# One step list per tile rewritten, one more filler product behind each early burst, one weight load issued elsewhere

## The chip, the cores and the metric

The kernel runs on one core of a Trainium2 chip. Its metric is the time of one execution on the device in microseconds (us), taken as the median of several runs. A separate profiled execution gives the trace that is quoted here; its times count from the first instruction of the program.

A core has five engines that run side by side, each through its own instructions in order: PE (TensorE, matrix products; its weight loads are shown as PEld), DVE (VectorE), ACT (ScalarE), POOL (GpSimd) and SP, which here only issues DMAs. They meet at semaphores. PE writes to PSUM, in banks; DVE and ACT read PSUM and write SBUF.

## The reference

The first half is a linear-attention recurrence with decay, for 4 batches, 8 heads, 768 steps and head size 48. Per batch and head, with a 48x48 state:

```
y[t]  = r[t] @ (state + (u * k[t]) outer v[t])
state = w[t][:, None] * state + k[t] outer v[t]
```

The second half takes the 3072 tokens by 384 features that come out of it through a two-layer network: `gelu(x @ w_in) @ w_out`, with 2048 hidden features and the exact gelu. The inputs r, k, v, w, u are float32; w_in and w_out are float64 and are reduced to float32 on the chip.

## The kernel before

**Tiles.** The 3072 tokens are cut into eight tiles of 384. For each tile `attention(x, unit)` does the recurrence in chunks of 64 steps, and `mlp(x)` does the network. Both are Python generators: each `yield` ends a piece, a handful of instructions. A loop over x runs the pieces of tile x's attention beside those of tile x-1's network; after the eighth tile the last network runs alone.

**The order of work is written by hand.** No scheduler moves anything: instructions stand on each engine in the order in which the Python code emits them. `PLAN[x]` is a string with one letter per piece. For x = 0: `.` and `s` step the two units of tile 0's attention (unit 0 and unit 1, half of the heads each), `f` begins tile 1's attention, `c` steps the conversion of the weights, `l` the loads, `w` loads v of tile 1. From x = 1 on: `.` steps `mlp(x-1)`, `s` the rest of `attention(x)`, `f` the beginning of `attention(x+1)`, `l` the loads of the next tile, `c` the conversion (tile 1 only), `x` sums of the inputs of `mlp(x)`, and `w` sums of weights, on DVE. What a string leaves over is run at its end; a letter whose generator is used up does nothing.

**Tile 0.** Here no network runs yet. Each unit goes through six levels (h = 1, 2, 4, 8, 16, 32). At each, `products` (L473) puts a burst of 24 small products on PE, DVE copies the wanted part of the result to `a_sb` (L569, masked) and scales r and k in place for the next level (L540, L551). Behind most bursts `keep_warm(1)` (L235) issues one product of zeros, 512 columns in bf16, whose result nobody reads. Then come the transposes of k (L742), which ACT copies out (L755), the products k v (L792, `kv_ps`), the chain of states on DVE (L824, L819), the products inside a chunk (L845) and those with the states (L888), both into `y_ps`, the fences on DVE (L855, L858), and the copies to `xT` (L895, L911, L914), the network's input. Tile 1's first burst is L489. The network of tile 0 then begins at L1278.

**Weights.** The weights come in 16 pieces of 768 KB, the first eight of w_in. `weight_in(i)` loads piece i into one of five `raw` buffers: with a gate in three DMAs, each ahead of it on DVE a memset of one element (L217) that makes SP wait for DVE, and without one in a single DMA (L213). `conversion()` turns piece i into float32: three ACT instructions a piece, made one piece ahead (L343, L344, L346), a shift on DVE (L355) and an addition on DVE (L359); behind the addition it calls `weight_in(i + 3)`, but not for piece 0. Piece 3 is therefore loaded by the `l` letters of tile 0, at the end of their chain:

```
"l": chain(weight_in(0, True), islice(second, 5), weight_in(1, True), weight_in(2, True), second, weight_in(3, True)),
```

`second` is `load_second`: eight loads of tile 1's r, k and w (L177), each behind a DVE memset (L176) as well.

**Tiles 1 to 7.** The network of tiles 0 and 1 uses L1278 for its first layer; from tile 2 on it is L1066, in fewer products (a two-level scheme with sums of weights and of inputs, L972 to L980 and L989). The second layer is L1372 in tile 0's network and L1292 otherwise. Its results leave by ACT and DVE (L1281, L1283 gelu in tile 0's network; L1411, L1415 for the output). PSUM for the network is two banks that change places, so a product waits for the reader of the one before the last. Attention's bursts from tile 2 on are L641 and L632.

Of the kernel before, what the change touches and what calls it, by code (L numbers as in the profile page):

```python
# [36 lines left out]
NC_SP = 8  # L37
HALFWAY = 2
PLAN = {
    0: ".lls.....sslsc.lsslll.sl.sls.f.sl.lfscsl..sfss.lscfs.lscs.s.sssscl..ls...ssslll.l.cs...sw.ccff",  # L40
    1: (
        ".cswc.ccc.cccss.lc.ccscs..cc.cs.cclwcsc.ccssc.c.cccsccc..ssccc.c.lcls.cc.ccsc.w.clwscclccc"
        ".c.swcw.ss.ccs.lcsc..cwcccslccslff..w..fw.wfs..f..flffffffww"
    ),
    2: "...l...s..ws.swssswssss.sslsw...ssss.sssws.ll..ws.w..lw.sw.wl.sls.sls..lf.s....sf..f.f.xx.fxl.x.x",
    3: "l..sss..s.s..s.s....s...s.ssllss.sss.s.s.ss.l..lsss..sssss.sls.s..s......s..ls.llssf.sf.sflf.f.x.x..xxfffxf",
    4: "...s...lsl......s.s....sss..ssss..s..ss..s..s...llssslss....s.slss...s...sll.sl.s.sfs..fsf.ff..xl.x.xfffxffx",
    5: ".l..........ls.ss...s.sslls.ssss..ss.sls...sss..sssssl.ss.s..s.......s.lssll.sfsf.f.s.ff.x..x.xxxl",
    6: "sss.sls.....s......ls.s....s.sssssss..s.....s.ss....s.s.ssss.s.l.ss.l.ls.l...s.l.lslssf..s.ffs..lff.xx..xffxffx",
    7: "......s.s....s.s...s.ssssss...sss.ss...sss..ssss.s...ss.ww.ww.wwsw.ww.ww.ws.s.ss.s.ww.swww.swwwwwwww.wwww.www.xxxx.xxxxxx",  # L50
}


# [11 lines left out]
def kernel(  # L65
# [47 lines left out]
    def pair(name):  # L113
        return pools["d"].tile([128, 2, BANK], F32, name=name, tag="d")
# [56 lines left out]
    def load_second(dma):  # L171

        loaded[1] = [None, None]
        for i in range(SHARES):
            s = slice(i * 3 * ALL // SHARES, (i + 1) * 3 * ALL // SHARES)
            nc.vector.memset(bufs[1][:, s.start:s.start + 1], 0.0)  # L176
            dma.dma_start(out=bufs[1][:, s], in_=rkw[1, :, s])  # L177
            yield

    def load(x, dma):  # L180

        if x >= NX:
            return
        loaded[x] = [None, None]
        for i in (0, 2, 1):
            t = bufs[x % 2 if i == 0 else 1]
            for j in range(3):
                a = i * ALL + j * ALL // 3
                dma.dma_start(out=t[:, a:a + ALL // 3], in_=rkw[x, :, a:a + ALL // 3])
                yield  # L190
        load_v(x, dma)
        yield
# [12 lines left out]
    def weight_in(i, gate=False):  # L205

        if i < len(pieces):
            dst, src = pieces[i]
            raws[i] = cv.tile([128, PIECE], I64, name="raw", bufs=AHEAD) if wide else None
            if wide:  # L210
                dst = raws[i].rearrange("p (a c) -> p a c", a=dst.shape[1])
            if not gate:
                nc.sync.dma_start(out=dst, in_=src)  # L213
                return
            for a in range(dst.shape[1]):
                if wide:
                    nc.vector.memset(dst[:, a].bitcast(U32)[:, 0:1], 0)  # L217
                nc.sync.dma_start(out=dst[:, a], in_=src[:, a])
                yield
# [12 lines left out]
    def keep_warm(n):  # L232
        t = ps.tile([128, BANK], F32, name="warm", tag="mm", bufs=2)
        for _ in range(n):
            nc.tensor.matmul(t, lhsT=zeros[:, 0:128], rhs=zeros, start=True, stop=True)  # L235
# [81 lines left out]
    def conversion():  # L317

        i = converted[0]
        if i >= len(pieces):  # L320
            return
        converted[0] += 1

        prepare(i + HALFWAY)
        yield
        if wide:
            yield from finish(pieces[i][0], raws[i], *halfway[i])
        for _ in weight_in(i + 3) if i else ():
            pass

    def convert():
# [3 lines left out]
    def prepare(upto):  # L335
        if not wide:
            return
        for i in range(len(halfway), min(upto, len(pieces))):
            words = raws[i].bitcast(U32).rearrange("p (a b) -> p a b", b=2)
            lo, hi = words[:, :, 0], words[:, :, 1]  # L340
            f = cv.tile([128, PIECE], U32, name="f")
            e = cv.tile([128, PIECE], U32, name="e")
            nc.scalar.activation(out=f.bitcast(F32), in_=hi.bitcast(F32), func=AF.Abs, scale=2.0 ** -112)  # L343
            nc.scalar.activation(out=e.bitcast(F32), in_=lo, func=AF.Identity, scale=2.0 ** -51, bias=two)  # L344
            sign = e.bitcast(F16).rearrange("p (a b) -> p a b", b=2)[:, :, 1]
            nc.scalar.activation(out=sign, in_=hi.bitcast(F32), func=AF.Copy, scale=2.0 ** -100)  # L346
            halfway.append((f, e))

    def finish(dst, raw, f, e):

        nc.vector.tensor_scalar(out=f, in0=f, scalar1=3, scalar2=None, op0=ALU.logical_shift_left)  # L355
        yield
        yield
        f, e = (z.rearrange("p (a c) -> p a c", a=dst.shape[1]) for z in (f, e))
        nc.vector.tensor_tensor(out=dst.bitcast(U32), in0=f, in1=e, op=ALU.add)  # L359
# [4 lines left out]
    def attention(x, unit):  # L364
# [101 lines left out]
        def products(bs, right, width, rest=False, last=False):  # L466
            d = pair("d")
            n = 0
            for b in bs:
                for i in range(NI):  # L470
                    for g in range(2):
                        for p in range(2):
                            nc.tensor.matmul(d[half[p], g, n * width:(n + 1) * width],  # L473
                                             lhsT=kc[half[g], b, i, p], rhs=right(half[g], b, i, p),
                                             start=True, stop=True)
                    n += 1
            if x == 0 and not rest and not last:
                keep_warm(1)
            return d[:, :, 0:n * width]

        def first_and_diagonal():
# [409 lines left out]
        if split:  # L891
            for c, copy in enumerate((nc.scalar.copy, nc.vector.tensor_copy)):
                for z in range(2):
                    s = slice(z * G, z * G + D)
# [5 lines left out]
        for b in reversed(range(np_)):  # L900
            for q in reversed(range(Q)):
# [5 lines left out]
                if which < NJ:  # L907
                    for z in range(2):
                        s = slice(z * G, z * G + D)
# [37 lines left out]
    def homes():  # L947

        more = [cv.tile([128, PIECE], I64, name="s", tag="raw", bufs=AHEAD).bitcast(F32) for _ in range(2)]
        s3_sb.append(more[0][:, 0:HF * 128].rearrange("p (f c) -> p f c", f=HF))  # L950
        x_sums.extend(z[:, i * HT:(i + 1) * HT] for z in (more[0][:, HF * 128:], more[1][:, HF * 128:]) for i in range(2))
        spare = [cv.tile([128, PIECE], F32, name=name) for name in ("f", "f", "e", "e")]
        for i, name in enumerate(("s1", "s2")):
            s12_of[name] = [z[:, 0:FG * 128].rearrange("p (f c) -> p f c", f=FG) for z in spare[2 * i:2 * i + 2]]
        s_both.extend((more[1], s_home))
        spare15.extend(z[:, FG * 128 + i * 128:FG * 128 + (i + 1) * 128] for z in spare[:1] for i in range(2))
        second = [more[1][:, i * WI:(i + 1) * WI] for i in range(HK)]
        third = [s_home[:, i * WI:(i + 1) * WI] for i in range(HK)]
        fourth = [z[:, FG * 128:] for z in spare]
        s_of.extend((second, third, fourth))  # L960
# [460 lines left out]
    second = load_second(nc.sync)  # L1421
# [8 lines left out]
    def next_v():  # L1430
        load_v(1, nc.sync)
        yield
# [7 lines left out]
    for x in range(NX):  # L1440
        if x == 2:
            homes()
        following = attention(x + 1, 0) if x + 1 < NX else iter(())
        if x == 0:
            streams = {
                ".": units[0], "s": units[1], "f": following, "c": pieces_of_w, "w": next_v(), "x": iter(()),
                "l": chain(weight_in(0, True), islice(second, 5), weight_in(1, True), weight_in(2, True), second, weight_in(3, True)),
            }
        else:
            streams = {  # L1450
                ".": mlp(x - 1), "s": slots, "f": following,
                "l": load(x + 1, nc.sync),
                "x": sums_of_x15(x) if x == NX - 1 else sums_of_x(x) if x > 1 else iter(()),
                "w": masks_and_sums() if x == 1 else chain(first_sum(), h_sums()) if x == 2 else sums_of_w15() if x == NX - 1 else iter(()),
                "c": pieces_of_w if x == 1 else iter(()),
            }
        for c in PLAN[x]:
            next(streams[c], None)
        for c in ".slxw" if x == 0 else ".slxwc":
            while next(streams[c], streams) is not streams:  # L1460
                pass
        slots = following
        if x == 1:
            fewer_pairs()
# [62 lines left out]
```

## Time and profile before

| What | us |
|---|---|
| Runs before | 586.98, 587.47, 590.91; median 587.47 |
| Profiled execution, its own time | 587.83 |
| Its span, first to last instruction | 585.9 |
| PE busy, of the span | 569.6 (97%) |
| DVE busy | 460.9 (79%) |
| ACT busy | 287.3 (49%) |
| PE busy in the first 30 us | 21.97 |
| PE busy from 30 to 60 us | 25.42 |
| First product of tile 0's network (L1278) | starts at 45.41 |

Some 1.9 us of the profiled execution's time lie outside its span. In a row of a timeline the columns are start, duration (both us), engine, line, operation, output<-input, shape and count; what stands in brackets is the idle time before the row and what ended it. "issue" there means that the engine waited for nothing that the profile shows. In a row of stretches the columns are the stretch, its length, the busy time of PE, PEld, DVE, ACT and POOL (instructions in brackets), the granted PE clock, the DMA engines' busy share, and GB/s. A float32 product is two rows of PE and two of PEld.

### The profile page before, as it was taken

To read this page: it belongs to the slowest core of one execution; us is meant where nothing else is said; L and a number is where in the kernel's file an instruction comes from. 1 tells how busy PE (TensorE), PEld (TensorE's weight loads), DVE (VectorE), ACT (ScalarE), POOL (GpSimd) and SP (SyncE) were. 2 spreads that over 40 slices of the span, in tenths; PEclk is the share of its full clock that TensorE was granted. 3 is DMA by queue.
4 is the path that set the end of the run, shared out by engine and by line. 5 is a ranking of instruction groups with operands and counts; after the bars stand their busy time and mean duration, and the time that the engine had idled before them with its cause. 6 is when DMAs were issued, how large, how long until landed. Compare 5 with 4: busy or idle time off the path is not lost. (4 is left out here: it accounts for less than half of the span.)

```text
span 585.9 us, 17174 instructions
## 1 busy us (share of the span) xinstructions
PE 569.6 (97%) x7405; PEld 507.1 (87%) x7408; DVE 460.9 (79%) x823; ACT 287.3 (49%) x672; POOL 8.0 (1%) x21
## 2 busy tenths in 40 slices
PE   7769999999999999999999999999999999999997
PEld 4556666766899999999999999999999999999997
DVE  7879766999969986787859987598768998975532
ACT  2566889322722558146463368245562465623400
POOL 4100000000000000000000000000000000000000
PEclk9899999999999999999999999999999999999999
DMA  7659661120142301341023311430015200210000
GB/s 248 207 146 349 239 207 56 37 86 2 32 138 79 111 2 32 97 126 39 1 42 104 122 39 19 96 118 5 3 30 166 73 3 2 43 39 7 1 15 34
DMA packets 51034, 46.78 MB, mean 80 GB/s; under 512 B 31760, under 2 KB 36112, under 8 KB 50960
## 3 DMA queue, kind: packets, MB, share of 16 engines
q1 hardware_dynamic: 50864, 45.62, 25.6%
q8 instruction: 58, 0.95, 0.7%
q14 instruction: 16, 0.13, 0.1%
q10 hardware_dynamic: 96, 0.07, 0.1%
HBM read 36.24 MB, written 4.72 MB: 70 GB/s over the span
## 5 line engine op out<-in xcount | busy, mean ns | idle before, releaser
L1066 PE MATMUL h_ps<-xT,w_in_sb 128*128 128x192 f32 x408 | 81.3, 330 | 0.7 <-DVE o_sb L1415 0.6
L1066 PEld LDWEIGHTS h_ps<-xT,w_in_sb 128*128 128x128 f32 x408 | 67.8, 190 | 3.7 <-ACT g L1098 1.2
L1278 PE MATMUL h_ps<-xT,w_in_sb 128*128 128x384 f32 x192 | 64.2, 490 | 0.1
L1278 PEld LDWEIGHTS h_ps<-xT,w_in_sb 128*128 128x128 f32 x192 | 35.8, 190 | 24.4 <-ACT rkw L1283 0.6
L1292 PE MATMUL o_ps<-w_out_sb,g 128*128 128x192 f32 x224 | 39.5, 326 | 0.0
L1292 PEld LDWEIGHTS o_ps<-w_out_sb,g 128*128 128x128 f32 x224 | 37.0, 190 | 0.3
L657 ACT COPY a_sb<-d 32x256 f32<-32x256 f32 (+8 forms) x90 | 32.6, 362 | 4.6 <-PE d L641 3.1
L1292 PE MATMUL o_ps<-w_out_sb,f 128*128 128x192 f32 x176 | 31.7, 330 | 0.0
L1292 PE MATMUL o_ps<-t,g 128*128 128x192 f32 x176 | 31.4, 329 | 0.0
L1292 PE MATMUL o_ps<-w_out_sb,e 128*128 128x192 f32 x176 | 31.3, 328 | 0.0
L1292 PE MATMUL o_ps<-t,e 128*128 128x192 f32 x176 | 30.9, 327 | 0.0
L1292 PE MATMUL o_ps<-t,s 128*128 128x192 f32 x176 | 30.9, 327 | 0.0
L1066 PE MATMUL u_ps<-s,w_in_sb 128*128 128x192 f32 x160 | 29.5, 327 | 0.0
L674 DVE COPY_PREDICATED a_sb<-quarter,d 128x480 f32<-128x480 uint8 (+5 forms) x54 | 23.2, 438 | 7.7 <-PE d L641 6.5
L1281 ACT ACTIVATE g<-h_ps 128x256 f32<-128x256 f32 (+1 forms) x32 | 13.8, 433 | 31.0 <-PE h_ps L1278 30.6
L1292 PEld LDWEIGHTS o_ps<-t,g 128*128 128x128 f32 x176 | 28.7, 190 | 0.4
L1292 PEld LDWEIGHTS o_ps<-w_out_sb,e 128*128 128x128 f32 x176 | 28.8, 190 | 0.3
L1292 PEld LDWEIGHTS o_ps<-w_out_sb,f 128*128 128x128 f32 x176 | 28.7, 190 | 0.4
L1292 PEld LDWEIGHTS o_ps<-t,s 128*128 128x128 f32 x176 | 28.8, 190 | 0.1
L1292 PEld LDWEIGHTS o_ps<-t,e 128*128 128x128 f32 x176 | 28.8, 190 | 0.1
L473 PEld LDWEIGHTS d<-rkw 64*64 64x64 f32 x1056 | 18.7, 142 | 11.2 <-issue 7.1
L641 PE MATMUL d<-kx,rkw 64*64 64x96 f32 x1056 | 28.2, 248 | 0.0
(247 smaller groups left out, 1185.6 us busy)
## 6 DMA issues: line engine op xcount, KB each, us to landing
rkw<-in_rkw_dram SPq DMA_DIRECT2D x54, 256.0 KB, 4.0
raw<-in_w_out_dram SPq DMA_DIRECT2D x8, 768.0 KB, 5.3
v_in<-in_v_dram SPq DMA_DIRECT2D x8, 584.0 KB, 4.0
out_dram<-o_sb SPq DMA_DIRECT2D x20, 192.0 KB, 1.9
rkw<-kx SPq DMA_DIRECT2D x72, 48.0 KB, 2.0
raw<-in_w_in_dram SPq DMA_DIRECT2D x12, 256.0 KB, 4.5
raw<-in_w_in_dram SPq DMA_DIRECT2D x4, 768.0 KB, 9.4
rkw<-in_rkw_dram SPq DMA_DIRECT2D x6, 384.0 KB, 5.5
```

Of the source, the lines that this page charges most:

```text
L473: nc.tensor.matmul(d[half[p], g, n * width:(n + 1) * width], lhsT=kc[half[g], b, i, p], rhs=right(half[g], b, i, p), start=True, stop=True)
L641: nc.tensor.matmul(o[half[p], i * 3 * C // 2:(i + 1) * 3 * C // 2], lhsT=kc[half[g], n // NI, n % NI, p], rhs=rx[half[g], 2 * n + p], star ...
L657: nc.scalar.copy(out=at[z, g, first:behind, (a + 1) * h:], in_=d[z, :, :, to] if g == slice(None) else d[z, :, to])
L674: nc.vector.copy_predicated(out=an[:, :, :, :, (a + 1) * h:], mask=mask.to_broadcast(data.shape), data=data)
L1066: nc.tensor.matmul(o, lhsT=lhsT, rhs=rhs, start=start, stop=True, skip_group_check=True)
L1278: nc.tensor.matmul(h_ps, lhsT=w_in_sb[:, f // FI, j, f % FI * 128:(f % FI + 1) * 128], rhs=xT[:, j, :], start=(j == 0), stop=(j == NJ - 1))
L1281: nc.scalar.activation(out=gs[group][:, f % FG, 0:t], in_=h_ps[:, 0:t], func=AF.Gelu)
L1292: nc.tensor.matmul(o, lhsT=lhs(j), rhs=rhs(j), start=start and j == 0, stop=(j == HF - 1), skip_group_check=True)
```

## The change

Three things change. `keep_warm(1)` in `products` becomes `keep_warm(2)`, for the ten bursts of tile 0 that had one. The load of weight piece 3 leaves the `l` chain and is issued, without a gate and in a single DMA, behind the addition of piece 0. All eight strings of `PLAN` are new: in tile 0 the letters but `l` stand as before and the last `l`s stand together and earlier; in tiles 1 to 7 the same pieces stand in another order, and the strings have a few letters more, which run what the end of the string ran before or do nothing.

```diff
 PLAN = {
-    0: ".lls.....sslsc.lsslll.sl.sls.f.sl.lfscsl..sfss.lscfs.lscs.s.sssscl..ls...ssslll.l.cs...sw.ccff",
+    0: ".lls.....sslsc.lsslll.sl.sls.f.sl.lfscsl..sfss.lscfs.lscs.s.ssssclll..s...sss..cs...sw.ccff",
     1: (
-        ".cswc.ccc.cccss.lc.ccscs..cc.cs.cclwcsc.ccssc.c.cccsccc..ssccc.c.lcls.cc.ccsc.w.clwscclccc"
-        ".c.swcw.ss.ccs.lcsc..cwcccslccslff..w..fw.wfs..f..flffffffww"
+        ".c.scccl..lscssc.cccscxcl..ccc.cscclcccc..ccscs.ccc.cc.ccss.cccccs.c.wcwccssss..c.ccss.ccl"
+        ".sswwww.cccccccslwcclllf....sslc...cc...sf.fs.ffff...fffwffwwwwwlc"
     ),
-    2: "...l...s..ws.swssswssss.sslsw...ssss.sssws.ll..ws.w..lw.sw.wl.sls.sls..lf.s....sf..f.f.xx.fxl.x.x",
+    2: "....s...slw.sswssl.sssss...ss.sss.swsllsslwsww...s...sl..www.wslss..lcs.s.lf.sl..fx.w.xxx....sxxfff.....l",
...
@@ conversion
-        for _ in weight_in(i + 3) if i else ():
+        for _ in weight_in(i + 3):
             pass
@@ products
             if x == 0 and not rest and not last:
-                keep_warm(1)
+                keep_warm(2)
@@ streams of x == 0
-                "l": chain(weight_in(0, True), islice(second, 5), weight_in(1, True), weight_in(2, True), second, weight_in(3, True)),
+                "l": chain(weight_in(0, True), islice(second, 5), weight_in(1, True), weight_in(2, True), second),
```

More of the change, by code (lines that the diff above doesn't have):

```diff
@@ L39 @@
 PLAN = {
-    0: ".lls.....sslsc.lsslll.sl.sls.f.sl.lfscsl..sfss.lscfs.lscs.s.sssscl..ls...ssslll.l.cs...sw.ccff",
+    0: ".lls.....sslsc.lsslll.sl.sls.f.sl.lfscsl..sfss.lscfs.lscs.s.ssssclll..s...sss..cs...sw.ccff",
     1: (
-        ".cswc.ccc.cccss.lc.ccscs..cc.cs.cclwcsc.ccssc.c.cccsccc..ssccc.c.lcls.cc.ccsc.w.clwscclccc"
-        ".c.swcw.ss.ccs.lcsc..cwcccslccslff..w..fw.wfs..f..flffffffww"
-    ),
-    2: "...l...s..ws.swssswssss.sslsw...ssss.sssws.ll..ws.w..lw.sw.wl.sls.sls..lf.s....sf..f.f.xx.fxl.x.x",
[L46 to L50, printed above, removed]
+        ".c.scccl..lscssc.cccscxcl..ccc.cscclcccc..ccscs.ccc.cc.ccss.cccccs.c.wcwccssss..c.ccss.ccl"
+        ".sswwww.cccccccslwcclllf....sslc...cc...sf.fs.ffff...fffwffwwwwwlc"
+    ),
+    2: "....s...slw.sswssl.sssss...ss.sss.swsllsslwsww...s...sl..www.wslss..lcs.s.lf.sl..fx.w.xxx....sxxfff.....l",
+    3: (
+        "wscl..ss..s..sss....s...l.s.ssssssss..s..l.ss...sss..sllssss.ss...s...s...s...sllsssllf.sl"
+        ".ff.fxxlx.xx....sffxfff"
+    ),
+    4: (
+        "......llls..ss.....s....sss..ssss.....llssss..s...ssss...s..lssc..ss.....ssllsss..lfs..lfs"
+        ".f..sffx..x.xffxxwfff.xl"
+    ),
+    5: ".......s...l.lls.s...s..ssssslssss...ss....sss.ssssss...s...ss...l.s..lslllfsss..c.sfffs..l..lwfxxx.xxx.",
+    6: (
+        "ss.ss....s...s....ss...s...sssls.slss....sss...s...ssss..lss...s..sscw....lll.ssll..sssslf"
+        "..sf.f.ffll.x..x.x.ffsffxxx"
+    ),
+    7: (
+        "......s..s...s.s...sss.ss.ss.sss..ss...wwwsss..swssswcs.ss.ww....l.s.wwwsww.wwww..ws.s.ss."
+        "s.wwwwwswwwwww.ww.xxxxxww..xxx.wwsxx.x"
+    ),
 }
```

## The prediction

> **What bounds the kernel.** I read the busy times first, then PE in thirty-microsecond stretches, since PE is busy for 97% of the span.
>
> ```profile
> PE 569.6 (97%) x7405; PEld 507.1 (87%) x7408; DVE 460.9 (79%) x823; ACT 287.3 (49%) x672; POOL 8.0 (1%) x21
> 0.00:30.00 30.00, 21.97 (x651) 15.09 (x654) 24.23 (x69) 12.42 (x20) 7.99 (x21) 0.94 0.69 227
> 30.00:60.00 30.00, 25.42 (x563) 18.37 (x562) 25.83 (x67) 20.60 (x42) 0.00 (x0) 1.00 0.74 253
> 60.00:90.00 30.00, 30.00 (x366) 18.85 (x365) 20.99 (x26) 26.14 (x45) 0.00 (x0) 1.00 0.59 202
> ```
>
> Of PE's 16.3 us without work, 12.6 lie before 60 us (8.03 + 4.58). From the start of tile 0's network (45.41) on, PE is full, and PE's list of waits from 60 us on has one line, 0.6 us behind the output's copies. So products can't be packed closer in tiles 1 to 7: their seven strings can lose time, and gain next to none. What can be gained lies before 45.41, and it moves the rest as a block. The second reading is therefore PE's timeline there.
>
> ```profile
> 36.47 0.39 PE L888 MATMUL y_ps<-rkw,st 64*64 64x64 f32 x5
> 38.19 1.09 PE L888 MATMUL y_ps<-rkw,st 64*64 64x64 f32 x30 [1.33 <-issue]
> ...
> 40.42 1.32 PE L888 MATMUL y_ps<-rkw,st 64*64 64x64 f32 x38 [0.27 <-DVE fence L855]
> ...
> 41.64 0.33 PE L489 MATMUL d<-kx,rkw 64*64 64x96 f32 x3
> 43.29 2.19 PE L489 MATMUL d<-kx,rkw 64*64 64x96 f32 x91 [1.32 <-issue]
> 45.41 0.91 PE L1278 MATMUL h_ps<-xT,w_in_sb 128*128 128x384 f32 x2
> ```
>
> Two stops with the word "issue" break rows that are otherwise back to back, in the middle of a group with its operands ready. A third stands in L473 (17.2 to 18.85, 1.42). Counted from the start of PE's rows, the three restarts are rows 703, 1727 and 1983: multiples of 256 apart. The queue that the page calls "instruction" moves records of 16 KB, and one ends 1.3 us before each restart (16.24 + 1.36, 35.92 + 0.96, 41.05 + 0.95). So I read them as PE out of instructions: a record follows PE's passing of a multiple of 256 and brings the next block but one. How long it takes hangs on the data. Block edges were passed at 28.06, 33.54 and 38.19; the records after the last two came 2.4 and 2.9 us later, and the DMA queues show why for the last:
>
> ```profile
> q1 hardware_dynamic: 529, 0.99, 92.2%
> q8 instruction: 1, 0.02, 5.9%
> ```
>
> The first line is 38.1 to 41 us, where the data queue alone appears; the second, from 41 to 42, is the record. Elsewhere, with quiet DMA engines, the record came 1.1 to 1.3 us behind the edge.
>
> **The load of piece 3.** It removes three DVE memsets (L217, 0.06 each) and two of three issues on SP, and takes 768 KB out of the time after 36.89, where SP issues them now:
>
> ```profile
> 36.89 1.33 SPq L218 DMA_DIRECT2D raw<-in_w_in_dram  x3
> 30.98 5.82 SPq L177 DMA_DIRECT2D rkw<-in_rkw_dram  x3
> ```
>
> It comes to stand on SP behind piece 2 and behind DVE's addition of piece 0 (29.98 to 30.93), with no wait for a buffer, five being there for the first five pieces. The `second` loads of the lower row now go at 30.98, 32.94 and 36.47; with the `l`s together they go at about 31. Piece 3 and the last of these, 0.77 + 0.29 MB at the 345 GB/s of 38.19 to 41, are 3.1 us of DMA. From 28.06 to 33.54 the engines are busy 48%, so 2.85 us are free, and 1.86 more up to 36.5. They fit, and 38.19 to 43.3 grows quiet.
>
> *Second stop* (41.64 to 43.29). The edge at 38.19 with a quiet record is 1.2 + 1.0 + 1.3 = 3.5 us, so 41.7, when PE is at that row: the stop goes. Without it L489's row follows 41.64 by some 0.09 instead of 1.65: −1.56. What is late next: the network waits for `xT` (L895 on ACT, ends at 43.43) and its DMAs, and L489's own rest (2.19) still covers that.
>
> *First stop* (36.86 to 38.19). The edge at 33.54 with a quiet record: 33.54 + 3.5 = 37.0, just in time; but that window now takes part of the moved bytes. And what follows is held by DVE: L888 of unit 0 needs the fences behind the state chain (L819, until 38.96), so it starts at 39.3 at best against 40.42, −1.1. Ends 0 and −1.1; I take the middle, −0.55, since the bytes end within a microsecond of that record.
>
> Sum of the load: **−2.1**. Ends 0 and −2.7, and a loss (the slower rival).
>
> **The second zero product.** Ten rows of 512 columns in bf16, 0.215 us each start to start at full clock, are 2.15 us of PE. They stand behind bursts after which PE waits for DVE or ACT (0.5 to 0.9 us: L551, L569, L566, L540 in PE's list of waits), so these waits hide them: 0. Uncovered it is +2.15. They could also earn: the clock was granted at half once, right behind a stretch of the same length in which PE worked 1.40 of 3.41 us.
>
> ```profile
> 15.97:19.38 3.41, 1.40 (x50) 1.01 (x49) 3.37 (x7) 3.26 (x5) 0.85 (x1) 1.00 0.52 130
> 19.39:22.80 3.41, 3.41 (x98) 2.80 (x97) 2.78 (x7) 1.10 (x4) 0.00 (x0) 0.50 1.02 342
> ```
>
> At half clock three bursts took 1.56, 1.51 and 1.39 instead of 0.93, 1.7 us in all, and DVE waited 0.36 + 0.54 + 0.64 for them. But two more zero rows there are 0.43 us, and the stop at 17.2, most of the idleness, has its record in flight already. And the gain wouldn't arrive: ACT stands until 25.64 for weight piece 1.
>
> ```profile
> 25.64 0.94 ACT L343 ACTIVATE f<-raw 128x768 f32<-128x768 f32 x1 [5.16 <-DMA raw<-in_w_in_dram]
> ```
>
> From there ACT goes nearly without pause (the conversion, L417/L419, eight L566 to 32.57, L755) to the products k v at 33.13. So I take 0; ends −1.5 and +2.15.
>
> [...] The ten products are also 20 more PE rows, so the edges fall up to 20 rows earlier in the work: about 0.3 us in a stop's favour, within the ends.
>
> **Plans 1 to 7.** Products and their number are the same; what changes is which piece stands ahead of which. *Tile 1:* ACT carries the conversion (three instructions, 2.8 to 3.0 us a piece, rows 35.34 to 38.25) besides gelu (L1281, 0.44), and PE takes six rows of L1278 per hidden block (64.2 us over 192 rows), 2.0 us. In the new order one more conversion stands ahead of a gelu whose bank PE wants two blocks later; 2.9 + 0.44 against the 4.0 of two blocks leaves cover, but where ACT is late already a little is lost: **+0.15**, ends 0 and +1.5 (half a conversion uncovered). *Tiles 2 to 7:* the distance on PE from a tile's products k v to the next tile's first burst, in products of 0.326 us, is 94, 114, 90, 86, 86, 86 before and 100, 110, 90, 86, 86, 86 now. Twice the change puts more products between the output's copies and the bank's next use, where the 0.6 us of waits are, so some 0.4 can go; DVE's spare time at the seam of tiles 2 and 3 falls from 1.2 us to about none. **−0.2**, ends −1.1 and +0.7.
>
> **Sum.** 587.83 − 2.1 + 0 + 0.15 − 0.2 = 585.7 against the profiled execution's own time (span 585.9 and 1.9 around it), which is 0.36 above the runs' median of 587.47. I state **585.6**.
>
> **Rivals.**
> 1. *The stops stay* as they are, since the data's bytes were not what delayed the records: only the strings' terms are left, 587 to 588.3. For it speaks that stops also occur at 17.2 with DMA engines busy but 52%. Against it the 92.2% and 1.1 to 1.3 us elsewhere. [...]
> 2. *The clock's gain arrives too*, or both stops go entirely: a further 1.1 to 2.1, 583.5 to 584.5.
> 3. *Slower: the moved bytes delay the earlier record.* With 3.1 us pushed into 28 to 36.5, the block after 33.54 comes later than 38.19. It decides once that record starts after 35.92. At the 2.9 us seen under 92% it starts at 36.45, +0.5, and with piece 3's tail still there up to 1.7 more at both stops: 588.3 to 589.5.
> 4. *Tile 1 starves:* gelus behind conversions uncovered by half a conversion or more at two or more blocks, +1.5 to +4: 589.5 to 592.
>
> **Chances.** Forecast (584.5 to 586.9) 50%, no gain 20%, clock 10%, late record 12%, tile 1 8%. The range takes the first four but for the tails: 583.6 to 589.0. A measurement of this kernel tells about 1% from no change, 5.9 us. All gains together (2.7 + 1.5 + 1.1) end below that, so faster by over 1% has 2%; slower by over 1%, above 593.3, needs tile 1 to starve and a lost seam, 6%; within 1%, 92%.
>
> **What would show it.** After the change, from PE's timeline: no "issue" row in L489, and one below 0.7 us or none in L888; L1278's first row at 43.0 to 43.8 instead of 45.41; the data queue below half from 38 to 41 us. Zero products: the same share of waits by DVE and ACT less 0.2 each, and one window at half clock still. From 60 us on: waits of PE below 1 us. I am wrong if L1278 starts at 45 or later, if the stops move to other rows with their length kept, or if PE's waits after 45 us pass 1.5 us.

## The result, and the profile after

The changed kernel takes 586.07 us (median of 14 runs, 584.17 to 587.45) against 587.75 (14 runs) for the kernel before beside it: a ratio of 0.9968, 95% interval 0.9953 to 0.9984, or 1.9 us less (0.9 to 2.8). Measured again it took 585.31 against 587.55: 0.9949 (0.9928 to 0.9970). Its profiled execution took 586.0, its span 584.1. New code stands 12 lines further down: L473 is now L485, L888 L900, L489 L501, L792 L804, L1278 L1290.

First the busy times and the thirty-microsecond stretches of the changed kernel, in the columns of before.

```profile
PE 570.4 (98%) x7418; PEld 505.7 (87%) x7418; DVE 460.1 (79%) x820; ACT 286.8 (49%) x672; POOL 8.1 (1%) x21
0.00:30.00 30.00, 23.18 (x660) 13.77 (x660) 22.94 (x66) 11.87 (x19) 8.11 (x21) 1.00 0.68 221
30.00:60.00 30.00, 26.44 (x575) 19.02 (x568) 26.40 (x62) 21.24 (x44) 0.00 (x0) 1.00 0.78 275
60.00:90.00 30.00, 30.00 (x456) 19.26 (x457) 21.04 (x27) 29.36 (x50) 0.00 (x0) 1.00 0.55 185
```

PE has 1.21 and 1.02 us more work in the first two stretches, and the granted clock of the first went from 0.94 to 1.00. ACT is busier by 3.2 us in the third, with 50 instructions for 45: in tile 1's new string its work comes sooner. Next, PE's timeline of the changed kernel around the two stops that the prediction counted on.

```profile
36.13 0.85 PE L804 MATMUL kv_ps<-v_in,g 64*64 64x48 f32 x43
38.23 0.26 PE L804 MATMUL kv_ps<-v_in,g 64*64 64x48 f32 x3 [1.24 <-issue]
...
40.91 1.32 PE L900 MATMUL y_ps<-rkw,st 64*64 64x64 f32 x37 [0.49 <-DVE fence L867]
...
42.14 2.18 PE L501 MATMUL d<-kx,rkw 64*64 64x96 f32 x94
44.25 4.21 PE L1290 MATMUL h_ps<-xT,w_in_sb 128*128 128x384 f32 x12
```

The stop in L501 (L489 before) is gone. The one near 38 us is there with 1.24 instead of 1.33, now five rows from the end of the products k v (43 of 48 stand ahead of it) instead of five rows into L900: the ten zero products, ten rows of PE and ten of PEld, moved it. Tile 0's network starts at 44.25 instead of 45.41. That is 1.16 us; the span is shorter by 1.8, so another 0.6 went after the start. The DMA queues of the changed kernel, from 28.06 to 33.54 and then from 38.1 to 41 us:

```profile
q1 hardware_dynamic: 696, 1.34, 79.0%
```

```profile
q8 instruction: 1, 0.02, 2.0%
```

and SP's issues:

```profile
29.04 0.43 SPq L225 DMA_DIRECT2D raw<-in_w_in_dram  x1
32.11 1.29 SPq L189 DMA_DIRECT2D rkw<-in_rkw_dram  x3
```

The bytes went where the prediction put them: the data queue has 79% of the earlier stretch (48% for all queues before) and nothing from 38.1 to 41, where only an instruction record is left (92.2% of data before). Two stretches around the place of the clock's fall, and ACT's wait for weight piece 1, in the changed kernel:

```profile
15.97:19.38 3.41, 2.26 (x87) 1.59 (x87) 3.41 (x8) 1.53 (x2) 1.97 (x4) 1.00 0.67 199
17.33:20.74 3.41, 2.18 (x71) 1.42 (x74) 3.41 (x7) 2.86 (x4) 0.75 (x1) 1.00 0.69 172
```

```profile
26.23 0.93 ACT L355 ACTIVATE f<-raw 128x768 f32<-128x768 f32 x1 [3.95 <-DMA raw<-in_w_in_dram]
```

The first stretch is the one that the prediction shows for before; the second counts in steps of 3.41 us, the length of the stretch at half clock in the profile of before, from the moment at which the clock of this execution first became whole (7.09). PE worked 2.26 instead of 1.40 us of the first, 2.18 of the second, and the clock stayed whole. ACT's wait ended 0.6 us later than before (25.64), but the first burst came 1.3 later as well (9.76 against 8.50): counted from there the wait ended 0.7 us sooner. From 60 us on, PE's list of waits has one line, and the output's copies aren't in it:

```profile
PE d L653 <- ACT a_sb L669: 0.2, 1, 0.2
```

### The profile page after: what moved, and what is told of

Its sections match the earlier page's. It is cut to its first block, busy times and chain, and to the rows that moved or that the text cites. A ratio compares the mean times of both kernels' runs of the same rounds, so it can differ in the third digit from the quotient of the medians.

```text
span 584.1 us, 17192 instructions
## 1 busy us (share of the span) xinstructions
PE 570.4 (98%) x7418; PEld 505.7 (87%) x7418; DVE 460.1 (79%) x820; ACT 286.8 (49%) x672; POOL 8.1 (1%) x21
## 4 chain that ended last, share of the span: by engine, by line
PE 93%; DMA 2%; ACT 2%; DVE 1%; issue 1%; SPq 0%; DVEq 0%; ACTq 0%
PE o_ps L1304 35%; PE h_ps L1078 16%; PE u_ps L1078 12%; PE h_ps L1290 11%; PE d L653 4%; PE o_ps L1384 4%; PE kv_ps L804 2%; PE y_ps L857 2%; PE y_ps L900 2%; PE c_ps L1078 2%; PE d L485 2%; DMA rkw<-in_rkw_dram 1%; DMA raw<-in_w_in_dram 1%; PE d L644 0%; ACT a_sb L669 0%
## 5 line engine op out<-in xcount | busy, mean ns | idle before, releaser
L1290 PE MATMUL h_ps<-xT,w_in_sb 128*128 128x384 f32 x192 | 64.3, 491 | 0.0
L1290 PEld LDWEIGHTS h_ps<-xT,w_in_sb 128*128 128x128 f32 x192 | 35.7, 190 | 24.6 <-ACT rkw L1295 0.9
L485 PEld LDWEIGHTS d<-rkw 64*64 64x64 f32 x1056 | 17.3, 135 | 12.5 <-issue 6.9
```

The costliest lines, as they stand in the source:

```text
L485: nc.tensor.matmul(d[half[p], g, n * width:(n + 1) * width], lhsT=kc[half[g], b, i, p], rhs=right(half[g], b, i, p), start=True, stop=True)
L1290: nc.tensor.matmul(h_ps, lhsT=w_in_sb[:, f // FI, j, f % FI * 128:(f % FI + 1) * 128], rhs=xT[:, j, :], start=(j == 0), stop=(j == NJ - 1))
```

## The experiments

All were timed in five rounds beside the kernel before. "Start" below is the first row of tile 0's network on PE, "first burst" the first row of L473 behind the first loads. The table at the end of this section has them for all kernels.

**Load alone**: the kernel before, with only this (and tile 0's string):

```diff
-        for _ in weight_in(i + 3) if i else ():
+        for _ in weight_in(i + 3):
-                "l": chain(..., weight_in(2, True), second, weight_in(3, True)),
+                "l": chain(..., weight_in(2, True), second),
```

> The kernel before with the load of weight piece 3 moved, and tile 0's string with it; one zero product, old strings for tiles 1 to 7. Theory (the data's bytes delay PE's instruction records): the stop in L489 is gone, the record behind the edge at about 38 us comes 1.1 to 1.3 us after it instead of 2.9, and tile 0's network starts 1.1 to 1.6 us earlier than before relative to PE's first burst; time 1.0 to 1.6 us below before. Rival (the stops are not delayed by data; the 20 more PE rows of the zero products moved the edge to a place without a stop): both stops keep their length, time within 0.5 us of before.

Measured: ratio 1.0003 (0.9985 to 1.0021). The stop in L489 is gone, and the other stop is 0.78; but the time did not fall. The record behind the edge at 38.59 came 1.13 us after it, as the theory has it. The theory was right on the stop and missed on the time; the rival was right on the time and missed on the stop.

**Zero products alone**: `keep_warm(1)` becomes `keep_warm(2)`.

> The kernel before with two zero products behind each early burst and nothing else changed. Theory (they neither cost nor earn at the end): the clock stays at 1.00 around 19 to 23 us, but ACT still waits for weight piece 1 until about 26, the stop in L489 stays at 1.3, tile 0's network starts where it did, within 0.3 us; time within 0.5 us of before. Rival A (the zeros moved the block edge and so removed the stop): time 1 us or more below. Rival B (the zeros hold PE up): up to 1.5 us above.

Measured: 1.0002 (0.9989 to 1.0016), clock 1.00 throughout the profile. The stops stay, but with 0.55 and 0.32. PE's waits after 50 us name something that the profile of before hadn't got:

```profile
PE h_ps L1278 <- ACT rkw L1283: 0.6, 1, 0.6
PE h_ps L1066 <- DVE o_sb L1415: 0.5, 1, 0.5
```

The start was at 43.34, 2.1 us before that of before; then, at 50 us, PE waits 0.6 for ACT's gelu of tile 0's network, in tile 1's string. That old string doesn't use this early start in full. The theory was right on the clock and the time, and missed on the stop in L489 and on the start.

**Strings of tiles 1 to 7 alone**: tile 0, its string, the load and the zero products as before.

> The kernel before with the new strings for tiles 1 to 7 alone. Theory: from the first row of tile 0's network to the end 0.6 us less, as the traces of before and after have it (540.5 against 539.85), PE without a wait for the output's copies; time 0.4 to 0.8 us below before. Rival (these 0.6 us are scatter between two profiled executions): within 0.2 us of before.

Measured: 0.9972 (0.9955 to 0.9989), 1.65 us less. This is more than the theory had, and most of what the whole change gains in its first measurement. From the start to the end of the span it takes 539.7 us, against 540.5. The two stops of this kernel, whose tile 0 is that of before:

```profile
37.83 1.09 PE L900 MATMUL y_ps<-rkw,st 64*64 64x64 f32 x30 [0.52 <-issue]
42.38 2.19 PE L501 MATMUL d<-kx,rkw 64*64 64x96 f32 x91 [0.77 <-issue]
```

The same code that stopped for 1.33 and 1.32 in the profile of before stopped for 0.52 and 0.77 here. One profile doesn't give the length of such a stop.

**Tile 0's part alone**: load and zero products new, strings of tiles 1 to 7 old.

> Load of piece 3 moved and two zero products, with the strings of before for tiles 1 to 7. Theory: the load's gain and the zeros' nothing add up, 1.0 to 1.6 us below before and 0.4 to 0.8 above the whole change. Rival (load and zeros act on each other, the 20 rows bringing the earlier stop into the products k v, ahead of DVE's state chain): 0.5 us or more above the load alone.

Measured: 0.9983 (0.9964 to 1.0003), about 1 us less and not clear of nothing. The start is at 44.09, but the rest takes 541.5 instead of 540.5: PE's waits have 0.6 for L1283 and 0.7 for the output's copies. What tile 0 gave, the old strings lost in part. The stop near 38 us stands in the products k v, as the rival has it, but the time is 1.2 us below the load alone, where the rival had 0.5 or more above it.

**Tile 1's string alone, and those of tiles 2 to 7 alone.**

> The kernel before with the new string for tile 1 alone. Theory (tile 1's old string makes PE wait for ACT's gelu only when tile 0's network starts early; kernels with the old string and a start at 43.3 to 44.4 us had 0.3 to 0.6 us of PE's L1278 waiting for ACT's L1283): that wait is absent, and from the start of tile 0's network to the products k v of tile 2 it is 118.5 us, as with all new strings; time 0 to 0.5 us below before. Rival (the whole gain of the strings is in tile 1): 1.2 to 2 us below.

> The kernel before with the new strings for tiles 2 to 7 alone. Theory: from the products k v of tile 2 to those of tile 7 it takes 343.6 us as with all new strings, against 344.2 to 344.7 with the old ones; time 0.6 to 1.0 us below before. Rival (tile 1 holds the gain): within 0.3 us of before.

Measured: 0.9983 (0.9964 to 1.0002) for tile 1's, and 1.0006 (0.9987 to 1.0026) for the others. With tile 1's new string the wait for L1283 is absent and the way from the start to the first product k v of tile 2 is 118.46 us, as expected. (With the old one and the old string of tile 2 it was 118.46 after the late start of before, and 118.8, 119.1 and 119.1 after the earlier ones of the first, second and fourth experiment.) With the strings of tiles 2 to 7 alone, the way from the products k v of tile 2 to those of tile 7 is 343.4, as expected; but at 130 us, in the network of tile 1 that tile 2's string steps, there is this, on PE and ahead of it on ACT:

```profile
PE h_ps L1290 <- ACT g L1293: 1.5, 1, 1.5
128.19 1.34 ACT L622 COPY kx<-rkw 128x384 f32<-128x384 f32 x3 [3.08 <-DVE rkw L452]
```

The gelu that PE waits for stands on ACT behind three copies, and these waited 3.08 us for DVE. With all new strings (the third experiment) the same copies run at 125.64 without a wait. So the new string of tile 2 behind the old one of tile 1 has a loss of 1.5 us at their seam that the full set hasn't. In the times the two theories missed: tile 1's string took 1.0 us off, more than the 0.5 at most, and the other strings nothing, which is what their rival has. Added up the two give 0.6 us against 1.65 for all seven, but the intervals, of 1 us to each side, don't exclude that they simply add. Neither part alone is shown to be faster, both together are.

**One zero product** in the changed kernel: `keep_warm(2)` goes back to `keep_warm(1)`; done twice, the second time beside a second run of the changed kernel.

> The changed kernel with one zero product behind a burst instead of two. Theory (zeros shorten the time from weight piece 1's conversion to tile 0's network, since all three profiles with two of them have no stretch at half clock and 17.9 to 18.0 us between the two, and those with one have 18.4 to 19.8): half clock returns, 0.5 to 1 us above the changed kernel. Rival (as predicted, ACT's wait hides the clock): within 0.3 us of it. In both, no stop in L501.

> The changed kernel with one zero product once more. Theory (the second one costs 1.3 us): 2.5 to 3.5 us below before. Rival (the first result was a low draw): 1.5 to 2 below, as the changed kernel.

> The changed kernel once more, beside the others of this call. It should give 1.5 to 2 us below before, 0.9 to 1.6 above the kernel with one zero product, with stops of 0.8 to 1.3 near 38 us in L804 and none in L501.

Measured: 0.9947 (0.9929 to 0.9965) and 0.9940 (0.9921 to 0.9959), with medians of 584.73 and 584.70; the changed kernel beside the second 0.9949 (0.9928 to 0.9970). The theory of the first expectation, that half clock would cost 0.5 to 1 us, fell: half clock was back in the first profile (clock 0.997; 1.000 in the second), and the time was lower, not higher. The second time is 3.5 us below before, where its theory had 2.5 to 3.5. The changed kernel again is 3.0 us below, more than the 1.5 to 2 expected. The second zero product thus earned nothing that is seen here; it may cost 0.5 to 1.2 us (0.0009 and 0.0021 of the ratio), but the intervals overlap, and side by side the two kernels' medians differ by 0.6 only.

**Old load and old tile 0 string** in the changed kernel:

> The changed kernel with piece 3 loaded where it was, and tile 0's old string. Theory (the load only trades the stop in L501, gone, for a longer one near 38 us, 1.24 instead of 0.5): within 0.4 us of the changed kernel, the stop near 41 to 43 us back with 0.3 to 1.3. Rival (as predicted, the load earns 1 us or more): 1 us or more above the changed kernel.

Measured: 0.9978 (0.9961 to 0.9996). The stop is back, and the earlier one is 1.51:

```profile
37.39 0.26 PE L804 MATMUL kv_ps<-v_in,g 64*64 64x48 f32 x3 [1.51 <-issue]
42.21 0.27 PE L900 MATMUL y_ps<-rkw,st 64*64 64x64 f32 x2 [0.87 <-issue]
```

Against the changed kernel's two measurements the load earns 0.6 and 1.7 us; with one zero product (third against seventh experiment's ratios, 0.9972 and 0.9947 or 0.9940) 1.5 and 1.9. Neither the theory's 0.4 at most nor the rival's 1 at least is excluded by the first pair; the second speaks for the rival.

**Two halves**: the zero products of the bursts cut to two of 256 columns, the rows of two and the time of one.

```diff
...
-            nc.tensor.matmul(t, lhsT=zeros[:, 0:128], rhs=zeros, start=True, stop=True)
+            nc.tensor.matmul(t[:, 0:cols], lhsT=zeros[:, 0:128], rhs=zeros[:, 0:cols], ...)
...
-                keep_warm(2)
+                keep_warm(2, BANK // 2)
```

> The changed kernel with its two zero products of 512 columns cut to two of 256: the rows of two, the time of one. Theory (the second product's 20 rows move the edge of PE's instruction blocks, so that the stop near 38 us falls into the products k v, ahead of DVE's state chain, and that is what the second product costs): the stop stands in L804 as in the changed kernel, and the time is the changed kernel's, 0.9 us or more above the one with one zero product. Rival (the second product's own time is what it costs): the time is that of one zero product, 0.9 us or more below the changed kernel.

Measured: 0.9958 (0.9936 to 0.9979), 585.26, beside 0.9949 (585.31) for the changed kernel and 0.9940 (584.70) for one zero product. It is apart from neither: undecided. The place of the stop came as expected. First this kernel, then the one with one zero product:

```profile
36.53 0.26 PE L804 MATMUL kv_ps<-v_in,g 64*64 64x48 f32 x3 [0.87 <-issue]
```

```profile
37.24 1.09 PE L900 MATMUL y_ps<-rkw,st 64*64 64x64 f32 x30 [1.00 <-issue]
```

Rows, not time, placed the stop: twenty rows more, ten of them PE's, moved it from five rows of PE into L900 to five before the end of the products k v.

**Edges moved**: one zero product behind a burst, and the 16 ahead of the first burst cut to 98 small ones.

```diff
...
-    keep_warm(16)
+    keep_warm(98, 84, 64)
...
-                keep_warm(2)
+                keep_warm(1)
```

> The changed kernel with one zero product, and with the 16 zero products ahead of the first burst cut to 98 small ones (84 columns, 64 rows out) of about the same time together: 164 more rows of PE, so every block edge falls 164 rows earlier in the work. Theory (a stop is there only where PE comes to an edge less than about 4.5 us after the edge before): the edge that is passed at 34.2 with one zero product is passed near 30, before PE's waits, and the stop of 1.07 in L900 is gone or below 0.3, with none in L501; tile 0's network starts 0.5 to 1.1 us earlier against the conversion of weight piece 1, and the time is 0.3 to 1.1 us below the kernel with one zero product. Rival (the stops are not tied to edges every 256 rows): the stop stays in L900 with about 1 us.

Measured: 0.9990 (0.9969 to 1.0011), 587.4, 2.7 us above one zero product. The stop near 38 us is gone and none is in L501, as the theory has it and the rival not. The theory's 4.5 us is an estimate; up to 100 us in the profiles of before and after, the six stops of 0.85 to 1.42 us stand at edges that PE reached 3.0 to 4.2 us behind the one before, and none stands at an edge that it reached later than that. The gain is not there; in the profile an earlier edge now falls in the time of the first loads. (This execution took 588.97, 1.6 us above the median of its runs, so what follows is at its worst here.) PE's, DVE's and ACT's timeline in turn:

```profile
15.67 0.51 PE L485 MATMUL d<-rkw 64*64 64x64 f32 x19 [4.00 <-issue]
...
38.74 1.56 PE L857 MATMUL y_ps<-a_sb,v_in 64*64 64x64 f32 x48
```

```profile
24.48 0.06 DVE L229 MEMSET raw<- 128x1 uint32 x1
```

```profile
28.87 0.94 ACT L355 ACTIVATE f<-raw 128x768 f32<-128x768 f32 x1 [5.07 <-DMA raw<-in_w_in_dram]
```

A stop of 4.00 us holds PE, so DVE behind it, so the last of the three memsets that let SP load weight piece 1; the piece lands at 28.87 instead of some 25.5, and the start moves to 46.84. With the stop near 38 gone the way from that landing to the start is still 17.97 (17.84 and 17.77 with the stop): L857 ran at half clock, 1.56 instead of 0.93.

| Kernel | first burst | start | from burst to start | from start to the span's end | ratio |
|---|---|---|---|---|---|
| before | 8.50 | 45.41 | 36.9 | 540.5 | 1 |
| load alone | 8.73 | 44.44 | 35.7 | 540.6 | 1.0003 |
| zeros alone | 8.91 | 43.34 | 34.4 | 541.0 | 1.0002 |
| tile 0's part | 9.70 | 44.09 | 34.4 | 541.5 | 0.9983 |
| tile 1's string | 8.90 | 44.06 | 35.2 | 540.8 | 0.9983 |
| strings 2 to 7 | 8.90 | 43.85 | 35.0 | 541.6 | 1.0006 |
| strings alone | 8.99 | 44.51 | 35.5 | 539.7 | 0.9972 |
| old load | 8.76 | 44.51 | 35.8 | 539.5 | 0.9978 |
| one zero product | 9.89; 8.60 | 44.22; 42.82 | 34.3; 34.2 | 539.3; 539.5 | 0.9947; 0.9940 |
| two halves | 8.55 | 42.55 | 34.0 | 539.5 | 0.9958 |
| edges moved | 9.11 | 46.84 | 37.7 | 540.2 | 0.9990 |
| changed | 9.76; 9.56 | 44.25; 43.86 | 34.5; 34.3 | 539.8; 539.6 | 0.9968; 0.9949 |

The columns of times, in us, are from single profiled executions, the ratio is from the runs. Load, zero products and the seven strings were timed in all their eight combinations. The mean of the four ratios with the new strings less that of the four with the old ones is −0.0034, or −2.0 us; for the load it is −0.0016, or −0.9 us, and for the second zero product nothing (+0.0001). By the intervals of the single ratios each of these is uncertain by some 0.7 us, an estimate: the strings are clear of nothing, the load barely.

## Why the prediction was right and where it was wrong

The time (585.6 forecast; 586.07 and 585.31 measured), its sign and its range were right. Of the marks that the prediction named, L501 without a stop, the data queue from 38 to 41 us and PE's waits from 60 us on came as said; the stop near 38 us did not shrink below 0.7, and the network started at 44.25 and 43.86, later than the 43.0 to 43.8 given. One of the signs of being wrong came true by half: the stop near 38 us went to other rows with nearly its length (1.24 and 1.32 for 1.33). Over the eight combinations the load earned 0.9 us where the sum has 2.1, and the strings 2.0 where it has 0.05. The two errors cancelled, so that the total was right in good part by luck. The sum also isn't carried through: less the 0.36 that lie between the profile and the runs' median it gives 585.3, not 585.6.

**The strings, −0.05 in the sum: wrong, by size.** The table's fifth column begins behind tile 0. With all new strings it is 539.3 to 540.2 (eight profiles, mean 539.7), with all old ones 540.5 to 541.5 (four, mean 540.9): −1.25 us. In the runs the strings alone gave −1.65. The terms failed one by one. Tile 1 was costed at +0.15, as a loss by a later gelu; the runs showed the reverse. It is the old string that had a gelu late: in three of the four profiles with it that start earlier than before, PE waits 0.3 to 0.6 at 50 us. The profile of before, whose start was later than in all others but one, did not show it. The early start alone isn't the cause, for the fourth profile (strings 2 to 7, start at 43.85) has no such wait; there the conversion that stands on ACT ahead of that gelu begins at 46.53, against 47.40 in the profile of tile 0's part. That fourth one lost 1.5 us at the seam with tile 2 instead. The wait for the output's copies went as said (0.4 to 0.7 in four of the five profiles with old strings from tile 2 on, at most 0.5 in sum and mostly none with new ones). The opening claim that the seven strings "can lose time, and gain next to none", since PE was full, was the faulty step: a full PE still had 1.25 us in it. Some 0.5 of it are waits that other executions had than the one read: PE's idle time behind the start, without the tail, is 0.6 to 1.6 us in the four profiles with old strings (mean 1.05) and 0.4 to 0.9 in the eight with new ones (mean 0.55). The other 0.7 lie in time that the profile counts as busy, and where is open.

**The load, −2.1 in the sum: right in mechanism, too large, and moved about.** Data in the way of instruction records was right: in six profiles with the old load a stop of 0.32 to 1.32 stands in L489 or just ahead of it, in eight with the new load none. The record behind that edge came 1.97 to 2.86 us after it with the old load, and 1.13 to 1.39 with the new one (seven, without the moved edges). The −1.56 was read from one execution; the six average 0.77. The −0.55 for the earlier stop was wrong in sign: with the new load it averages 1.07 (the same seven, 0.78 to 1.32), with the old one 0.65 (six, 0 to 1.51). That is the third rival's mechanism: the moved bytes came to stand ahead of an earlier record, which came 2.10 us after its edge in the mean, against 1.70. Data isn't all of it there, as the profile of before has 2.38 with the data queue at 42.7% (33.5 to 35.9). The sum of the two stops is −0.35. From first burst to start the load gives −0.9 with one zero product (four profiles against three) and −0.7 with two (two against three). In the runs it gave nothing (1.0003) and 1.1 us (1.0002 against 0.9983, with two zero products) under the old strings, and 0.6 to 1.9 us under the new ones; these differ by no more than their intervals.

**The zero products, 0 in the sum: about right, for a wrong reason.** Against the forecast of one window at half clock still, the clock stayed whole in all five profiles with two of them, and fell in seven of the eight with one product of 512 columns. The five were a lucky draw: of all timed runs the clock was 1.000 in 38 of 62 with two products, and in 26 of 181 with one. So the second product often keeps the clock, which the forecast did not expect, but not always. In every profile the clock's changes lie whole multiples of 3.41 us apart (in that of before at 5.73, 19.39 and 22.80). Counted in such windows, up to 48 us, PE was busy for 0.96 to 1.83 us of the one ahead of each of the eight falls, and for 1.64 or more in each one behind which the clock stayed.

The size of 0 has more for it than the reason given. In the 101 runs of the kernel before beside the experiments, the 14 at 1.000 took 587.4 in the mean and the 48 at 0.997, which is one window at half clock (half of 3.41 us in 586), 587.6. (In the kernels with two products the like difference is 1.0, from 38 and 15 runs; whether the clock makes it is not shown.) The reason given for a gain of 0 was that ACT waits for weight piece 1 anyway. That wait is no fixed date: the run with moved edges shows piece 1's last gate on DVE behind PE's bursts, and ACT starting on the piece 4.4 us behind it. What PE wins early moves the landing too. Why the runs showed no gain beyond that is open. In the three profiles with both load and two full zero products the first burst comes at 9.56 to 9.76, elsewhere at 8.50 to 9.11 with one exception (9.89). The loads that it waits for are issued at the same times, to 0.1 us, and whether this is chance stays open; it would take back up to 1 us.

**The rivals.** "The stops stay": the earlier of the two did. Stops of 0.3 to 4.0 us stand in all profiles. The third rival, the late record, was there as a mechanism but not as a result: the 1.51 of it came with the old load too. "The clock's gain arrives" was half right: the clock was kept more often, and no gain is seen from the second product. "Tile 1 starves" was wrong for the new string; the old one showed waits of that kind, of 0.3 to 0.6 us.

## What to carry to other kernels

Where one profile has stops that come from contention, their lengths are one draw: the same tile 0 gave 36.9, 35.5, 35.2 and 35.0 us from first burst to start. Size a gain from several executions, or give it the whole spread. An order that fits one arrival time can be late for an earlier one: behind the old string of tile 1, three of four earlier starts of tile 0's network came with 0.3 to 0.6 us of PE waiting for gelu, behind the new one none did. So look behind a gain ahead of a tuned stretch for the waits that it opens. And where a change has a few parts, time all combinations: single differences of about 1 us were within their intervals here, and the means over the others told the parts apart.

The fastest kernel seen here is the change without its second zero product: 584.7 us, 0.9947 and 0.9940 of before, though not clear of the changed kernel itself.

## What the hardware did that was not expected

At the same row of the same code PE stopped for anything from nothing to 2.1 us (near 24 us, before and load alone), and for 4.00 us when the edge fell into the time of the first loads (record at 13.2 us, restart at 15.67). At the two edges between 33 and 39 us a record came 1.13 to 1.39 us behind its edge where no data moved, and up to 2.86 us where data did. The stops' place followed the count of rows: 20 more rows from products of half the length moved the stop by as many rows, and 164 more removed the one near 38 us. The clock was decided by little: with 1.64 to 1.83 us of PE work in a window of 3.41 it went either way, and a second zero product behind each burst kept it whole in 38 of 62 runs, where one did in 26 of 181.
